# Products that nobody reads, put into the waits of the first stage of a three-part kernel

## The chip, the cores and the metric

The kernel runs as one program on one core of one Trainium2 chip. The metric is the device time of one execution in microseconds (us). TensorE (PE) multiplies, VectorE (DVE), ScalarE (ACT) and GpSimd (POOL) work elementwise, SyncE (SP) issues nearly all DMAs. PE's clock has two levels, 1.2 and 2.4 GHz; the profile gives the granted clock as a share of the higher one, so 0.50 is the lower level.

## The reference

Three parts follow one another, each fed by the one before; all inputs and outputs are float32.

```python
# 1 recurrence: batch 4, heads 8, steps 768, width 48
a = (a_re + i*a_im) * min(|a|, 0.999) / (|a| + 1e-6)
S = a[t] * S + outer(k[t], v[t]);   y[t] = q[t] @ real(S)
# 2 x: 3072 tokens x 384, from y
x = ((x @ w_a) * (x @ w_b)) @ w_out          # 384 -> 1536 -> 384
# 3 routing: 8 experts of 384 -> 1024 -> 384; tokens with x @ w_skip > 0
e = argmax(x @ w_gate);  g = softmax(x @ w_gate)[e]
out = x + g * (relu(x @ w1[e]) @ w2[e])      # the other tokens: out = x
```

## The kernel before

Part 1 is worked in 24 units of 128 time steps of one batch (`units`). A unit has three pieces of code: `att_exp` (logarithm of the magnitude, its running sum as a product with a triangle, exponentials), `att_trig` (phase, its running sum `tp` by a product with a triangle in line 251, sine and cosine, scaled q and k), and `att_pe` (transposes of q and k to `pq` and `pk`, the products `pc`, masked by DVE to `sc`, the output `y` and the state step `ds`). Two units are one group `g` of 256 tokens, of which there are 12.

Part 2 works a group in 12 blocks of 128 hidden columns. `moe1_step(g, f)` is one block: 9 products with w_a and 9 with w_b of 128x128 by 256 columns into the two halves of one bank `ab` of PSUM (lines 506 to 508; tag `ab`, two banks, so a block needs the bank of the block two before it to be read out), then ACT, DVE, ACT and DVE make the two halves `gh` and `gl` of the product, and `moe1_out` adds the block to `op` (lines 490 to 492), two blocks later.

The weights of part 2 arrive in 18 chunks. `decode_w` turns a chunk into float32 (ACT line 378, DVE lines 379, 383, 384), lets POOL release the load of the chunk three further on (`load_after`, line 429), and splits it into a high and a low part (ACT line 389, POOL line 390). For each of the six chunks of w_out it also forms w_out times the gate weights, twice (x = 0, 1): three transposes into a bank `wt` (line 448), ACT copies them out as `wtt` (line 450), three products with the gate weights (line 452) write columns 384 to 394 of the same bank, and DVE copies those to `w2s` (line 453).

The first stage, up to about 150 us, mixes the first units of part 1, the decoding of all chunks and the 12 blocks of group 0. Its program order is the string `START` (`d` a chunk, `e` and `t` the two halves of `att_exps` and `att_trigs`, `m0.3` block 3 of group 0): 

```python
START = 'da0 e0 t0 db1 db0 a do0 da1 do1 m0.0 e1 m0.1 m0.3 da2 m0.2 t1 db2 do2 m0.5 da3 do3 m0.4 db3 da4 l2 m0.7 db4 m0.6 do4 m0.9 do5 m0.8 da5 db5 m0.10 b m1.0 m0.11 e2 t2 m1.4 ...'
```

From this order a planner at build time, with its own estimates of durations, writes the order of each engine: of the instructions that it takes for ready, the earlier traced goes first. `after(later, earlier)` only orders two instructions of one engine. Each engine then runs its list strictly in order; a group of PE products that waits holds up all behind it.

The kernel already has products that nobody reads: two in line 474 behind the first sines (tile `warm`), and in `warm()` (line 666) 10, 6, 24, 13 and 8 of 256 columns, all near 730 to 740 us between part 2 and part 3, made of the bf16 constants `ones` and `iota`.

Of the kernel before, what the change touches and what calls it, by code (L numbers as in the profile page):

```python
# [18 lines left out]
P = 128  # L19
# [30 lines left out]
FILLP = ()  # L50
WARMS = (10, 6, 24)
WARMX = (13, 8)
ENGINES = {getattr(mybir.EngineType, x) for x in ("PE", "Activation", "DVE", "Pool")}
GF = 5
SGN = ()
# [4 lines left out]
def kern(tc, q, k, v, a_re, a_im, w_a, w_b, w_out, w_skip, w_gate, w1, w2, out):  # L60
# [3 lines left out]
    with st:  # L64
# [8 lines left out]
        def bank(tag, name, bufs):  # L73
            return ps.tile([P, 512], F32, tag=tag, name=name, bufs=bufs)

        env = SimpleNamespace(at=("at", "at2"), n=0)

        def at(name):
            env.n += 1
# [157 lines left out]
        def att_trig(i):  # L237
            c, b = units[i]
            d = U[i]
            im = d["im"]  # L240
            t3 = ew.tile([P, W], F32, tag="t3", name=f"t3_{i}")
            t4 = ew.tile([P, W], F32, tag="t4", name=f"t4_{i}")
            tact(out=t4, in_=im, func=AF.Arctan)
            if c > 0:

                cr = ew.tile([1, W], F32, tag="cr", name=f"cr{i}", bufs=1)
                sync.dma_start(cr, carry[b])
                dve.scalar_tensor_tensor(out=t4[:1], in0=cr, scalar=-2.0 * math.pi, in1=t4[:1], op0=ALU.mult, op1=ALU.add)
            tp = at(f"tp_{i}")
            if i < SPL:  # L250
                pe.matmul(tp[:, :W], trit, t4, start=True, stop=True)
            else:
                hi, lo = parts(i, "t", ("t2", "t1"))
                act.activation(out=hi, in_=t4, func=AF.Copy, scale=INV2PI)
                dve.scalar_tensor_tensor(out=lo, in0=t4, scalar=INV2PI, in1=hi, op0=ALU.mult, op1=ALU.subtract)
                cumsum(tp, hi, lo)

            if i in OFF.get("magic", ()):
                act.activation(out=t3, in_=tp[:, :W], func=AF.Identity, bias=b_magic)
            else:  # L260
                dve.tensor_scalar(out=t3, in0=tp[:, :W], scalar1=MAGIC, scalar2=None, op0=ALU.add)
            dve.scalar_tensor_tensor(out=t3, in0=t3, scalar=MAGIC, in1=tp[:, :W], op0=ALU.subtract, op1=ALU.subtract)
            if c + 1 < NCH:
                carry[b] = dpool.tile([1, W], F32, name=f"carry{i}")
                sync.dma_start(carry[b], t3[127:128])
            dve.tensor_scalar(out=t4.bitcast(I32), in0=t3.bitcast(I32), scalar1=0x7FFFFFFF, scalar2=None, op0=ALU.bitwise_and)
            tact(out=t4, in_=t4, func=AF.Sin, scale=-TWO_PI_IN, bias=b_hpi)
            ts = ew.tile([P, W], F32, tag="t1", name=f"ts{i}")
            d["ts"] = ts
            marks["ts", i] = tact(out=ts, in_=t3, func=AF.Sin, scale=-TWO_PI_IN)  # L270
            for nm in ("q", "k"):
                tag = "krl" if nm == "k" and i >= 6 and i % 2 else nm + "r"
                r = ew.tile([P, 2 * W + 32], F32, tag=tag, name=f"{nm}r{i}", bufs=1)
                if nm == "k":
                    pool.memset(r[:, 2 * W :], 0.0)
                    d["kf"] = r
                r = r[:, : 2 * W].rearrange("t (h x d) -> t h x d", x=2, d=D)
                src = d[nm].rearrange("t (h d) -> t h d", d=D)
                off(nm + "c", i).tensor_tensor(out=r[:, :, 0], in0=src, in1=t4.rearrange("t (h d) -> t h d", d=D), op=ALU.mult)
                e = off(nm + "s", i)  # L280
                ins = e.tensor_tensor(out=r[:, :, 1], in0=src, in1=ts.rearrange("t (h d) -> t h d", d=D), op=ALU.mult)
                if e is dve:
                    mark((nm + "r", i), ins)
                d[nm + "r"] = r

        xts = {}

        def att_pe(i):
# [2 lines left out]
            qr, kr, vt, ee = d["qr"], d["kr"], d["v"], d["ee"]  # L291
            sc, qT = [], []
            stt = state[b]
            def delta(prev=None):

                ds = at(f"ds{i}")
                for h in range(H):
                    for x in range(2):
                        l = d["kf"][:, 96 * h + 64 * x : 96 * h + 64 * x + 64]
                        ins = pe.matmul(ds[64 * x : 64 * x + 64, h * D : (h + 1) * D], l, vt[:, h * D : (h + 1) * D], start=True, stop=True).ins  # L300
                        if prev is not None:
                            after(ins, prev)
                        prev = ins
                return ds, prev
# [9 lines left out]
            for hh in range(2):  # L314
                pq = at(f"pq{i}_{hh}")
                for j in range(4):
                    pe.transpose(pq[:96, j * P : (j + 1) * P], qr[:, 4 * hh + j].rearrange("t x d -> t (x d)"), ident)  # L317
                tq = ew.tile([96, 512], F32, tag="tq", name=f"tq{i}_{hh}", bufs=2)
                mark(("tq", i, hh), act.activation(out=tq, in_=pq[:96], func=AF.Copy))
                pk = at(f"pk{i}_{hh}")  # L320
                for j in range(4):
                    pe.transpose(pk[:96, j * P : (j + 1) * P], kr[:, 4 * hh + j].rearrange("t x d -> t (x d)"), ident)  # L322
                tk = ew.tile([96, 512], F32, tag="tk", name=f"tk{i}_{hh}", bufs=2)
                mark(("tk", i, hh), act.activation(out=tk, in_=pk[:96], func=AF.Copy))
                pc = at(f"pc{i}_{hh}")
                for j in range(4):
                    last = pe.matmul(pc[:, j * P : (j + 1) * P], tk[:, j * P : (j + 1) * P], tq[:, j * P : (j + 1) * P], start=True, stop=True).ins  # L327
                s_ = ew.tile([P, 4, P], F32, tag="sc", name=f"sc{i}_{hh}", bufs=2)
                msk = mark(("sc", i, hh), dve.tensor_tensor(out=s_, in0=pc.rearrange("s (j t) -> s j t", t=P), in1=tri[:, None, :].to_broadcast([P, 4, P]), op=ALU.mult))
                sc.append(s_)  # L330
                qT.append(tq)
# [37 lines left out]
            if c + 1 < NCH:  # L369
                new_state(ds)  # L370
            del U[i]


        def decode(dst, raw, by_pool, k):
# [57 lines left out]
        def decode_w(k, dec, wtp, ahead=None):  # L432
            nm, f = chunks[k]
            dd = dec(f"dec{nm}{f}")
            d = dd.rearrange("p (c f) -> p c f", c=2 if nm == "o" else NCC)
            decode(d, env.raw.pop((nm, f)), k in SGN, k)
            if ahead:
                load_after(k + ahead, dd)
            t = env.wpool.tile([P, 2, 2, WO] if nm == "o" else [P, 2, NCC, 2 * P], F32R, tag=f"w{nm}{f}", name=f"w{nm}{f}")
            env.w[nm, f] = t  # L440
            split(*((t[:, x, :, :DM] if nm == "o" else t[:, x] for x in range(2))), d)
            if nm != "o":
                return
            w2 = env.mp.tile([P, 2, 10], F32, tag="w2", name=f"w2s{f}", bufs=2)
            for x in range(2):
                pt = bank("at2", f"wt{f}_{x}", 2)
                for c in range(NCC):
                    pe.transpose(pt[:, c * P : (c + 1) * P], d[:, x, c * P : (c + 1) * P], ident)
                wt = wtp.tile([P, DM], F32, tag="cr", name=f"wtt{f}_{x}", bufs=1)
                act.activation(out=wt, in_=pt[:, :DM], func=AF.Copy)  # L450
                for c in range(NCC):
                    pe.matmul(pt[:, DM : DM + 10], wt[:, c * P : (c + 1) * P], wg[:, c], start=c == 0, stop=c == NCC - 1)
                dve.tensor_copy(w2[:, x], pt[:, DM : DM + 10])
            split(t[:, 0, :, DM:], t[:, 1, :, DM:], w2)

        def att_exps(p):
            table("natural_log_exp_and_others")
# [8 lines left out]
        def att_trigs(p):  # L466
            table("trig_and_small")
            for i in (2 * p, 2 * p + 1):
                att_trig(i)
            if p == 0 and WARM:  # L470

                wm = bank("op", "warm", 2)
                for x in range(WARM):
                    pe.matmul(wm[:, :DM], ident, U[0]["ts"], start=True, stop=True)
            for i in (2 * p, 2 * p + 1):
                att_pe(i)


        M = {}
# [18 lines left out]
        def moe1_step(g, f):  # L498
            xt = M[g][0]
            fs = slice((f % 2) * P, (f % 2 + 1) * P)  # L500
            ab = bank("ab", f"ab{g}_{f}", 2)
            for x, nm in enumerate("ab"):
                o = ab[:, x * 256 : (x + 1) * 256]
                for c in range(NCC):
                    wh, wl = (env.w[nm, f // 2][:, y, c, fs] for y in range(2))
                    pe.matmul(o, wl, xt[:, c, 0], start=c == 0, stop=False)  # L506
                    pe.matmul(o, wh, xt[:, c, 1], start=False, stop=False)  # L507
                    pe.matmul(o, wh, xt[:, c, 0], start=False, stop=c == NCC - 1)  # L508
            if len(pend) == 2:
                moe1_out(*pend.pop(0))  # L510
            asb = env.mp.tile([P, 256], F32, tag="asb", name=f"asb{g}_{f}")
# [146 lines left out]
            if last:  # L658
                warm("t", ins.ins, WARMS[2])

        def warm(name, ins, n):

            if n:
                wm = bank("op", f"warm{name}", 2)
                for x in range(n):
                    after(pe.matmul(wm[:, :CAP], ones, iota, start=True, stop=True).ins, ins)

        giu = cpool.tile([P, 2, NE], U32, name="giu")
        siu = cpool.tile([P, 2, NE], U32, name="siu")
# [241 lines left out]
        moe1_flush()  # L911
        att_next(2)
        env.at = ("at", "at2")
        for g in range(2, NG):
            if g + 1 < NG:
                att_exps(g + 1)
# [186 lines left out]
```

## Time and profile before

| | us |
|---|---|
| median of 3 runs | 890.77 |
| lowest, highest | 889.37, 890.77 |
| the profiled execution, its own time | 892.15 |
| span of its profile, first to last instruction | 890.2 |
| PE busy in the span | 832.7 (94%) |
| DVE, ACT, POOL busy | 560.0, 466.0, 268.3 |

The profiled execution took 1.95 us more than its span, and 1.4 us more than the median. "Idle before" with an arrow names what an engine waited for; L506 is line 506.

### The profile page before, as it was taken

The page shows a single profiled execution, that of the slowest core. Times are in us where ns is not written, and L with a number is a line of the kernel's source. Part 1 is how long each engine was busy: PE and PEld are TensorE (multiplying, and loading weights), DVE is VectorE, ACT ScalarE, POOL GpSimd, SP SyncE. Part 2 cuts the span into 40 slices and gives each one's busy share as a digit, 9 for nine tenths or more (in the row PEclk, how much of TensorE's full clock was granted, in tenths as well). Part 3 has the DMA queues.
Part 4 walks back from the last instruction along what each step waited for, and adds up shares of the span by engine and source line. Part 5 has one row for each costly group of instructions (what it writes and reads, how often), then busy time and mean ns, then how long its engine had stood idle before and what let it go on. Part 6 is the DMA issues. An engine that isn't in the chain of part 4 may idle for free.

```text
span 890.2 us, 18349 instructions
## 1 busy us (share of the span) xinstructions
PE 832.7 (94%) x7051; PEld 804.1 (90%) x7051; DVE 560.0 (63%) x1323; ACT 466.0 (52%) x971; POOL 268.3 (30%) x313
## 2 busy tenths in 40 slices
PE   2578888999999999999999999999999999999995
PEld 0458788999999999999999999999999989999995
DVE  3788986857758385674957749484653644755551
ACT  5576655645647375573745647265443424555540
POOL 5254464114130031310213121031301304676751
PEclk9987987999999999999999999999999999999998
DMA  9869672222223131230312213121101408777600
GB/s 164 162 128 176 158 138 55 72 43 74 47 64 63 28 82 37 72 64 19 90 39 65 60 33 89 33 60 22 55 1 55 133 36 307 244 219 230 194 20 30
DMA packets 162801, 81.53 MB, mean 92 GB/s; under 512 B 132789, under 2 KB 148731, under 8 KB 162705
## 3 DMA queue, kind: packets, MB, share of 16 engines
q1 hardware_dynamic: 160656, 74.88, 35.4%
q0 software_dynamic: 2048, 5.40, 1.7%
q8 instruction: 57, 0.93, 0.5%
q14 instruction: 40, 0.32, 0.1%
HBM read 66.10 MB, written 12.61 MB: 88 GB/s over the span
## 4 chain that ended last, share of the span: by engine, by line
PE 82%; DVE 7%; DMA 5%; ACT 2%; issue 1%; SPq 1%; POOL 1%; POOLq 0%; DVEq 0%; ACTq 0%
PE ab L506 11%; PE ab L508 11%; PE ab L507 11%; PE op L490 5%; PE op L491 5%; PE op L492 5%; PE pc L327 4%; PE y L349 4%; PE eh L783 3%; PE eh L784 2%; PE eh L786 2%; PE eo L800 2%; PE eo L802 2%; PE eo L801 2%; PE pq L317 2%; PE pk L322 2%
## 5 line engine op out<-in xcount | busy, mean ns | idle before, releaser
L506 PE MATMUL ab<-xt,wa 128*128 128x256 f32 x432 | 127.1, 294 | 3.0 <-POOL wa L390 1.2
L506 PE MATMUL ab<-xt,wb 128*128 128x256 f32 x432 | 123.6, 286 | 1.1 <-POOL v L181 1.1
L508 PE MATMUL ab<-xt,wa 128*128 128x256 f32 x432 | 124.1, 287 | 0.0
L507 PE MATMUL ab<-xt,wa 128*128 128x256 f32 x432 | 123.8, 287 | 0.0
L508 PE MATMUL ab<-xt,wb 128*128 128x256 f32 x432 | 123.5, 286 | 0.0
L507 PE MATMUL ab<-xt,wb 128*128 128x256 f32 x432 | 123.0, 285 | 0.0
L513 DVE TENSOR_TENSOR asb<-ab,asb 128x256 f32<-128x256 f32 x144 | 60.3, 418 | 87.8 <-ACT asb L512 86.8
L490 PE MATMUL op<-wo,gl 128*128 128x394 f32 x288 | 100.3, 349 | 2.4 <-DVE gl L517 1.7
L492 PE MATMUL op<-wo,gh 128*128 128x394 f32 x288 | 99.3, 345 | 0.0
L491 PE MATMUL op<-wo,gh 128*128 128x394 f32 x288 | 99.1, 344 | 0.0
L512 ACT ACTIVATE asb<-ab 128x256 f32<-128x256 f32 x144 | 54.2, 376 | 84.6 <-PE ab L508 83.0
L515 ACT ACTIVATE gh<-asb 128x256 fp32r<-128x256 f32 x144 | 59.8, 415 | 67.0 <-DVE asb L513 66.7
L506 PEld LDWEIGHTS ab<-xt,wa 128*128 128x128 f32 x432 | 83.6, 193 | 6.3 <-issue 2.0
L517 DVE TENSOR_TENSOR gl<-asb,gh 128x256 fp32r<-128x256 f32 x144 | 64.1, 445 | 34.3 <-ACT gh L515 34.3
L751 POOL TENSOR_TENSOR wq<-stg,wq 128x768 fp32r<-128x768 f32 x32 | 59.4, 1858 | 85.1 <-DMA xt<-xt 44.0
L507 PEld LDWEIGHTS ab<-xt,wa 128*128 128x128 f32 x432 | 83.8, 194 | 0.0
L508 PEld LDWEIGHTS ab<-xt,wa 128*128 128x128 f32 x432 | 83.6, 194 | 0.2 <-issue 0.2
L506 PEld LDWEIGHTS ab<-xt,wb 128*128 128x128 f32 x432 | 82.2, 190 | 1.7 <-POOL v L181 1.3
L508 PEld LDWEIGHTS ab<-xt,wb 128*128 128x128 f32 x432 | 82.2, 190 | 0.3 <-issue 0.3
L507 PEld LDWEIGHTS ab<-xt,wb 128*128 128x128 f32 x432 | 82.3, 190 | 0.2 <-issue 0.2
L790 DVE SCALAR_TENSOR_TENSOR hl<-eh,hh 128x256 fp32r<-128x256 f32 x64 | 27.1, 424 | 52.2 <-ACT hh L789 52.2
L789 ACT ACTIVATE hh<-eh 128x256 fp32r<-128x256 f32 x64 | 24.6, 384 | 66.8 <-PE eh L786 65.1
(231 smaller groups left out, 2177.1 us busy)
## 6 DMA issues: line engine op xcount, KB each, us to landing
stg<-in_moe_w_dram SPq DMA_DIRECT2D x28, 768.0 KB, 4.5
re<-in_a_re_dram SPq DMA_DIRECT2D x24, 192.0 KB, 2.7
v<-in_v_dram SPq DMA_DIRECT2D x24, 192.0 KB, 2.7
k<-in_k_dram SPq DMA_DIRECT2D x24, 192.0 KB, 3.3
q<-in_q_dram SPq DMA_DIRECT2D x24, 192.0 KB, 2.9
rawo<-in_moe_w_out_dram SPq DMA_DIRECT2D x6, 768.0 KB, 4.4
xd<-xr SPq DMA_DIRECT2D x24, 192.0 KB, 2.3
out_dram<-xr SPq DMA_DIRECT2D x24, 192.0 KB
```

The costliest lines, as they stand in the source:

```text
L327: last = pe.matmul(pc[:, j * P : (j + 1) * P], tk[:, j * P : (j + 1) * P], tq[:, j * P : (j + 1) * P], start=True, stop=True).ins
L490: pe.matmul(o, gl[:, ts], wh, start=f == 0, stop=False)
L491: pe.matmul(o, gh[:, ts], wl, start=False, stop=False)
L492: i = pe.matmul(o, gh[:, ts], wh, start=False, stop=f == NF - 1)
L506: pe.matmul(o, wl, xt[:, c, 0], start=c == 0, stop=False)
L507: pe.matmul(o, wh, xt[:, c, 1], start=False, stop=False)
L508: pe.matmul(o, wh, xt[:, c, 0], start=False, stop=c == NCC - 1)
L512: act.activation(out=asb, in_=ab[:, :256], func=AF.Copy)
L513: dve.tensor_tensor(out=asb, in0=ab[:, 256:], in1=asb, op=ALU.mult)
L515: act.activation(out=gh, in_=asb, func=AF.Copy)
L517: dve.tensor_tensor(out=gl, in0=asb, in1=gh, op=ALU.subtract)
L751: lo.tensor_tensor(out=o[:, 1], in0=t, in1=o[:, 0], op=ALU.subtract)
```

## The change

It adds products that nobody reads in four places and a flag `busy` that is on through the first stage only.

- Behind the phase sum of unit 1 (`tp`, line 251): 60 products of 256 columns in an `op` bank (`warm("c")`), traced ahead of `att_pe` of units 0 and 1.
- Behind the first transpose of unit 0: 40 products of the triangle with itself, 128 columns (`warm("d")`), traced behind all of `att_pe(0)`.
- In each of the 12 passes through line 448: 5 products of 112 columns into columns 400 to 512 of the `wt` bank behind the transposes, and 5 more behind the gate product.
- Ahead of blocks 0, 3 and 9 of group 0: 8, 12 and 10 products of 256 columns into the block's own `ab` bank. They are ordered behind `env.last`: the last product of the block traced before, and for block 0 the gate product of the first chunk of w_out.

Nothing is removed. `START`, the holds and all other code stay.

```diff
+WARMA = (60, 40)
+WARMT = (5, 5)
+WARMB = {'ab0': 8, 'ab3': 12, 'ab9': 10}
@@ decode_w
                 for c in range(NCC):
-                    pe.transpose(pt[:, c * P : (c + 1) * P], d[:, x, c * P : (c + 1) * P], ident)
+                    ins = pe.transpose(pt[:, c * P : (c + 1) * P], d[:, x, c * P : (c + 1) * P], ident).ins
+                if env.busy:
+                    fill(pt, WARMT[0], ins)
...
+                if env.busy:
+                    fill(pt, WARMT[1], ins)
+                    if f == 0:
+                        env.last = ins
                 dve.tensor_copy(w2[:, x], pt[:, DM : DM + 10])
...
+        def fill(b_, n, ins, col=400, w_=112):
+            for x in range(n):
+                after(pe.matmul(b_[:, col : col + w_], ones, iota[:, :w_], start=True, stop=True).ins, ins)
@@ att_trigs
             for i in (2 * p, 2 * p + 1):
-                att_trig(i)
+                ins = env.last = att_trig(i)
+            if p == 0:
+                warm("c", ins, WARMA[0])
...
-                att_pe(i)
+                ins = att_pe(i)
+                if i == 0:
+                    warm("d", ins, WARMA[1], tri_r, tri_r)
@@ moe1_step
             ab = bank("ab", f"ab{g}_{f}", 2)
+            if g == 0 and env.busy:
+                fill(ab, WARMB.get(f"ab{f}", 0), env.last, 0, 256)
...
-                    pe.matmul(o, wh, xt[:, c, 0], start=False, stop=c == NCC - 1)
+                    env.last = pe.matmul(o, wh, xt[:, c, 0], start=False, stop=c == NCC - 1).ins
```

## Rows read from the trace of the kernel before

**Rows 1.** The page, chain that ended last, shares by engine.

```profile
PE 82%; DVE 7%; DMA 5%; ACT 2%; issue 1%; SPq 1%; POOL 1%; POOLq 0%; DVEq 0%; ACTq 0%
```

**Rows 2.** Busy by stretch: PE, PEld, DVE, ACT, POOL; then clock, DMA share, GB/s.

```profile
150.00:850.00 700.00, 695.96 (x6128) 683.32 (x6127) 434.28 (x1125) 365.61 (x785) 178.38 (x202) 1.00 0.31 85
```

**Rows 3.** The same view cut where the granted clock changes in the first stage.

```profile
71.00:74.40 3.40, 1.46 (x13) 1.26 (x11) 3.40 (x4) 1.62 (x3) 2.03 (x2) 1.00 1.01 201
74.40:84.60 10.20, 8.52 (x40) 8.05 (x41) 10.16 (x23) 9.10 (x18) 3.89 (x5) 0.50 1.02 158
...
118.80:125.70 6.90, 5.79 (x27) 5.76 (x28) 6.87 (x9) 4.33 (x10) 6.90 (x6) 0.51 0.44 122
...
139.60:149.80 10.20, 9.47 (x38) 9.47 (x39) 5.39 (x11) 6.75 (x14) 6.54 (x10) 0.52 0.19 40
```

**Rows 4.** PE's instructions in order, 17 to 40 us: start, length, line, count, idle.

```profile
17.11 2.93 PE L251 MATMUL tp<-t,trit 128*128 128x384 f32 x4 [2.80 <-ACT t L153]
25.95 2.93 PE L474 MATMUL warm<-ts,ident 128*128 128x384 f32 x4 [5.91 <-ACT ts L153]
31.31 1.09 PE L317 MATMUL pq<-ident,qr 128*96 128x128 f32 x4 [2.43 <-DVE qr L279]
...
37.03 2.07 PE L327 MATMUL pc<-tq,tk 96*128 96x128 f32 x8 [2.67 <-ACT tk L324]
38.90 1.06 PE L322 MATMUL pk<-ident,kr 128*96 128x128 f32 x4
```

**Rows 5.** Waits of DVE and of ACT, 28 to 57 us: total, times, longest.

```profile
DVE sc L329 <- PE pc L327: 2.9, 1, 2.9
...
ACT tk L324 <- PE pk L322: 2.5, 1, 2.5
```

**Rows 6.** PE's instructions in order, 65 to 89 us.

```profile
65.86 0.55 PE L506 MATMUL ab<-xt,wa 128*128 128x256 f32 x1 [0.23 <-DMA xt<-xt]
...
67.28 0.87 PE L452 MATMUL wt<-wg,wtt 128*128 128x10 f32 x6
...
75.14 0.90 PE L448 MATMUL wt<-ident,deco 128*128 128x128 f32 x3 [2.68 <-DVE w2s L453]
...
79.72 0.56 PE L506 MATMUL ab<-xt,wa 128*128 128x256 f32 x1
...
87.31 1.05 PE L327 MATMUL pc<-tq,tk 96*128 96x128 f32 x8
```

**Rows 7.** DVE's instructions in order, 77 to 89 us.

```profile
77.32 0.41 DVE L513 TENSOR_TENSOR asb<-ab,asb 128x256 f32<-128x256 f32 x1
...
88.41 0.69 DVE L329 TENSOR_TENSOR sc<-pc,tri_r 128x512 f32<-128x512 f32 x1 [2.99 <-PE pc L327]
```

**Rows 8.** The chain that ended last, 84 to 140 us: start, length, what.

```profile
110.94 4.79 DMA rawb<-in_moe_w_b_dram
...
127.88 6.91 DMA rawa<-in_moe_w_a_dram
```

**Rows 9.** PE's instructions in order, 137 to 149 us.

```profile
137.23 0.84 PE L452 MATMUL wt<-wg,wtt 128*128 128x10 f32 x6 [1.75 <-ACT wtt L450]
...
140.33 0.70 PE L490 MATMUL op<-wo,gl 128*128 128x394 f32 x1 [1.65 <-DVE gl L517]
...
144.88 0.56 PE L506 MATMUL ab<-xt,wa 128*128 128x256 f32 x1
...
148.65 0.41 PE L508 MATMUL ab<-xt,wb 128*128 128x256 f32 x1
```

**Rows 10.** Instructions of POOL, SP's queue and ACT in order, 140 to 150 us.

```profile
140.93 1.85 POOL L390 TENSOR_TENSOR wa<-deca,wa 128x768 fp32r<-128x768 f32 x1 [0.77 <-ACT wa L389]
...
142.08 3.69 SPq L368 DMA_DIRECT2D xt<-xt  x6
...
149.16 0.38 ACT L512 ACTIVATE asb<-ab 128x256 f32<-128x256 f32 x1 [1.82 <-PE ab L508]
```

**Rows 11.** PE's products that nobody reads, between part 2 and part 3.

```profile
733.64 2.78 PE L666 MATMUL warmt<-iota,ones 128*128 128x256 bf16 x24
```

More of the change, by code (lines that the diff above doesn't have):

```diff
@@ L74, in bank @@
             return ps.tile([P, 512], F32, tag=tag, name=name, bufs=bufs)
-        env = SimpleNamespace(at=("at", "at2"), n=0)
+        env = SimpleNamespace(at=("at", "at2"), n=0, busy=True)
         def at(name):
@@ L250, in att_trig @@
             if i < SPL:
-                pe.matmul(tp[:, :W], trit, t4, start=True, stop=True)
+                last = pe.matmul(tp[:, :W], trit, t4, start=True, stop=True).ins
             else:
+                last = None
                 hi, lo = parts(i, "t", ("t2", "t1"))
@@ L284, in att_trig @@
                 d[nm + "r"] = r
+            return last
         xts = {}
@@ L293, in att_pe @@
             stt = state[b]
+            first = None
             def delta(prev=None):
@@ L316, in att_pe @@
                 for j in range(4):
-                    pe.transpose(pq[:96, j * P : (j + 1) * P], qr[:, 4 * hh + j].rearrange("t x d -> t (x d)"), ident)
+                    ins = pe.transpose(pq[:96, j * P : (j + 1) * P], qr[:, 4 * hh + j].rearrange("t x d -> t (x d)"), ident).ins
+                    first = first or ins
                 tq = ew.tile([96, 512], F32, tag="tq", name=f"tq{i}_{hh}", bufs=2)
@@ L371, in att_pe @@
             del U[i]
+            return first
         def decode(dst, raw, by_pool, k):
@@ L451, in decode_w @@
                 for c in range(NCC):
-                    pe.matmul(pt[:, DM : DM + 10], wt[:, c * P : (c + 1) * P], wg[:, c], start=c == 0, stop=c == NCC - 1)
+                    ins = pe.matmul(pt[:, DM : DM + 10], wt[:, c * P : (c + 1) * P], wg[:, c], start=c == 0, stop=c == NCC - 1).ins
+                if env.busy:
+                    fill(pt, WARMT[1], ins)
+                    if f == 0:
+                        env.last = ins
                 dve.tensor_copy(w2[:, x], pt[:, DM : DM + 10])
             split(t[:, 0, :, DM:], t[:, 1, :, DM:], w2)
+        def fill(b_, n, ins, col=400, w_=112):
+            for x in range(n):
+                after(pe.matmul(b_[:, col : col + w_], ones, iota[:, :w_], start=True, stop=True).ins, ins)
         def att_exps(p):
@@ L659, in slots, with warm @@
                 warm("t", ins.ins, WARMS[2])
-        def warm(name, ins, n):
+        def warm(name, ins, n, l=None, r=None):
             if n:
@@ L665, in warm @@
                 for x in range(n):
-                    after(pe.matmul(wm[:, :CAP], ones, iota, start=True, stop=True).ins, ins)
+                    o = wm[:, :CAP] if l is None else wm[:, :P]
+                    after(pe.matmul(o, ones if l is None else l, iota if l is None else r, start=True, stop=True).ins, ins)
         giu = cpool.tile([P, 2, NE], U32, name="giu")
@@ L913, in kern @@
         env.at = ("at", "at2")
+        env.busy = False
         for g in range(2, NG):
```

## The prediction

> **What bounds the kernel now.** I read the shares of the chain that ended last first: 82% of it is PE [rows 1]. The view by stretch then says where: from 150 to 850 us PE is busy 695.96 of 700 us at granted clock 1.00 [rows 2]. Whatever brings PE to its 150 us mark earlier is therefore kept to the end, and nothing before that mark counts unless it moves it. So the question is what sets the mark.
>
> The same view cut at the changes of clock shows three stretches at half speed: 74.4 to 84.6, 118.8 to 125.7 and 139.6 to 149.8 [rows 3]. Each follows a pause of PE: 2.68 us ahead of the transposes at 75.14 [rows 6], 1.65 us ahead of the products at 140.33 [rows 9]. A fourth shows in durations alone. The clock column has 1.00 for the first 50 us, but eight products `pc` take 2.07 us at 37.03 [rows 4] and 1.05 us at 87.31 [rows 6], so PE is at the lower level there too.
>
> Which of these are on the chain? At 88.41 DVE had waited 2.99 us for `pc` [rows 7], which PE reached late because it worked at half speed from 79.72. From there the chain goes over DVE to a load of weights at 110.94, then over ACT and POOL to a last load, begun at 127.88 and landed at 134.79 [rows 8], over DVE, and at 140.33 back to PE, which works 9.47 of 10.2 us at half speed [rows 3]. So half speed is paid in full at the end, partly around 80 us, and not at all at 118.8: there PE only has to be done before a load that lands at 134.79.
>
> **Prices.** 24 products of 256 columns that nobody reads took 2.78 us, the last of them 0.27 us in length, so one costs (2.78 - 0.27) / 23 = 0.109 us at full speed [rows 11]. At half speed the 18 products of a block start from 144.88 to 148.65, 0.22 us each [rows 9]. By columns, 112 cost 0.048 or 0.097 us and 128 cost 0.055 or 0.11 us (estimates).
>
> **Behind the first phase sums: 60 and 40.** The sums end at 17.11 + 2.93 = 20.04. PE then idles 5.91 us, runs the two old warm products, idles 2.43 us, and transposes at 31.31 [rows 4]. The cover is 8.3 us. The 60 cost 6.5 us at full and 13.2 us at half speed; the planner takes them ahead of the transposes, since they are traced first. How soon does the clock rise? The three stretches lasted 6.9 to 10.2 us [rows 3]; with the shortest laid from the start of the sums at 17.11, it rises at 24.0 (an estimate): 18 products at 0.22 and 42 at 0.109 end at 28.6, the two old ones then take half of 2.93, and at 30.1 PE is ahead of the transposes: nothing lost. If it never rose, they would end at 33.2 + 2.93 = 36.2, 4.9 us late. I take the first, since the sums already kept PE working for 2.93 us. The 40 products of 128 columns are traced behind all of `att_pe(0)`, so the planner puts them only where it sees PE idle; the pause ahead of `pc` is 2.67 us [rows 4], and they cost 2.2 or 4.4 us. Hidden at full speed; up to 1.7 us late at half.
>
> The gain: at full speed `pc` is 1.0 us and `pk` about 0.5 us shorter. ACT waited 2.5 us for that `pk` and DVE 2.9 us for `pc` [rows 5], so between 0 and 2.4 us can come out there. Of what comes out, ACT and DVE hand on a part. **-1.0 us** taken, bounds -2.4 and +4.9.
>
> **Around the transposes of the output weights: 12 times 5 and 5.** 120 products, 5.8 us at full and 11.6 us at half speed. They lie on two paths. On PE they matter only where PE is late. On the way from transposes over ACT to `w2s` they matter everywhere, because reading a bank waits for all products into it: ACT reads only the first half of `ab`, yet idled 1.82 us until 149.16, past the end of the last product into the second half at 149.06 [rows 9, 10]. So each pass is 0.24 us longer at ACT and 0.24 us at DVE (0.48 at half speed). Behind ACT's copy all its queue waits (the decoding and the splits of weights), behind DVE's copy the next decode step. Twelve passes in a stage where DVE is seldom idle would cost up to 5.8 us if all lay on the chain; the rows show PE's results waiting for DVE instead (the 2.68 us at 75.14 [rows 6]), so I take 0 here and count the two passes on PE's own path below.
>
> **Ahead of block 0: 8.** They are ordered behind the gate product at 67.28, while block 0 began at 65.86 [rows 6]. So block 0 starts later by 1.4 us and by the products' 0.9 to 1.8 us, less the gate product, which now goes first. Cover: the pause of 2.68 us ahead of 75.14, which ends with DVE, not PE. Cost 0; without cover 2.3 us. They also shorten that pause, after which the clock fell.
>
> **Ahead of block 3: 12.** They need the bank of block 0, which DVE has read at 77.32 + 0.41 = 77.73 [rows 7], and stand in front of 79.72 [rows 6], on the way to the `pc` for which DVE waits. Full speed from there saves half of 79.72 to 84.6, 2.4 us, and pays 12 x 0.109 = 1.3 and 0.24 for a pass: -0.9. If the clock rises at 84.6 as before, 12 of the block's own products move behind it: +1.3 and 0.24, +1.6. If the rise is put off by as much as is added, 12 x 0.22 and two fives at half speed: +3.6. Nothing in the trace decides between the first two; I take **0**, bounds -0.9 and +3.6.
>
> **Ahead of block 9: 10.** 1.1 or 2.2 us, before the stretch at 118.8 that the load at 127.88 covers. 0; 2.2 without cover.
>
> **The end of the stage.** Here the clock falls at 139.6, and PE had little to do ahead of it: a gate product at 137.23 behind a pause of 1.75 us, a few more products, a pause of 1.65 us [rows 9]. Two fives of the new products come into just this stretch, 0.5 us. If the clock holds, the work from 140.33 to 144.88 shrinks to 2.3 us, but block 10 needs POOL's part of its weights at 140.93 + 1.85 = 142.78 [rows 10]: 2.1 us won, then half of 144.88 to 149.8, another 2.4. Against that stands a five behind the gate product in this stretch, 0.24 us. So -4.3 us; less if the next block in PE's list is of group 1, whose `xt` is still being issued up to 142.08 + 3.69 = 145.77 [rows 10]: then some 2 us of it go into that wait, -2.3 us. If it doesn't hold: +0.5 us. I take **-3.6 us**, nearer to the larger, since the only wait that the rows show there is the one for 142.78.
>
> **Sum.** -1.0 + 0 + 0 + 0 - 3.6 = -4.6 us on the profiled execution's own 892.15: 887.55. The median lies 1.4 us below that execution, so 886.2 us.
>
> **Rivals.** (1) The clock at the end isn't held: ten short products are little in a stretch with 3.4 us of pauses, and at 71.0 to 74.4 PE was busy 1.46 of 3.4 us and the clock still fell [rows 3]. Then -1.0 + 0.5: 890.2 us. (2) The change doesn't do what it says: PE runs a list that the planner wrote by its own estimates, so the products may stand where PE was busy anyway, not in the pauses, and the clock falls as before; PE pays only what lies on its path at the end, 0.2 to 0.5 us: 891.2. (3) Slower: the products ahead of block 3 run at half speed and put `pc` off. Place: between DVE's read of block 0's bank at 77.73 and `pc`. It decides if the clock is low when that bank comes free and rises no sooner for it. Price +3.6, with the end not held +0.5 and the early gain of 1.0 kept: 893.9. For it: the clock was 0.50 from 74.4 [rows 3]. Against it: the later start of block 0 may put off that fall. (4) All half-speed time comes back.
>
> The three stretches hold 27.3 us, half of which is 13.7 us: 877.1 us. The chain speaks against it, as PE is not on it at 118.8. The Trainium skill (TensorE: Matmul & The Clock Gate, "HAM oscillation") counts it that way: the loss is the throttled time times one half. By that rule the sum would be these 13.7 us; the trace bears it out for the last stretch alone, where PE is busy 9.47 of 10.2 us.
>
> **How the numbers follow.** Forecast 0.48 (its own range 883.5 to 888.7), end not held 0.19, not what it says 0.06, slower 0.23, all comes back 0.04. A measurement of this kernel tells about 0.2% (1.8 us) from no change. Faster: the forecast, the last rival and a little of the first, 0.54; same: the rest of the first and the second, 0.23; slower 0.23. The range reaches from 882.5 (the forecast with -2.4 early, -0.9 at block 3 and -4.3 at the end comes to 883.2) to 893.5, which leaves out the last rival and about half of the slower case.
>
> **What would show it.** Right: a clock of 1.00 through 140 to 150 us and block 10 starting near 143; `pc` of the first unit in 1.05 us; no later transposes than 31.3. Wrong: the 60 still running past 30 us; products ahead of block 3 at 0.22 us each and DVE's wait for `pc` at 88 us above 3 us; the products standing next to busy work; or a load in [rows 8] issued later than before, since then an order changed that I took for unchanged.

## The result and the profile after

| kernel | median us | lowest to highest | ratio to before, 95% interval |
|---|---|---|---|
| before, beside it | 890.37 | 888.65 to 892.14 | |
| after | 900.10 | 894.13 to 901.35 | 1.0085 [1.0066, 1.0103] |

The change makes the kernel slower by 0.85%, 7.6 us by the ratio (the two medians lie 9.7 us apart; this text goes by ratios). The forecast was 4.6 us faster, and 900.1 lies above the range. The profiled execution of after took 898.64 us with a span of 896.7, against 892.15 and 890.2 before. One execution can lie some 6 us off its kernel's median (after itself has one at 894.13), so verdicts below go by the ratios and the profiles only show places.

The page of after, busy time and the chain by engine: PE gained 16.8 us of work, and the chain is PE's as in [rows 1].

```profile
PE 849.5 (95%) x7301; PEld 821.4 (92%) x7301; DVE 558.9 (62%) x1323; ACT 466.3 (52%) x971; POOL 269.0 (30%) x313
PE 83%; DVE 6%; DMA 5%; issue 2%; ACT 1%; POOL 1%; SPq 1%; POOLq 0%; DVEq 0%; ACTq 0%
```

After by stretch, at the cuts of [rows 3] and [rows 2] (columns as there; the clock is the third number from the end):

```profile
71.00:74.40 3.40, 3.40 (x20) 2.96 (x21) 2.93 (x4) 1.70 (x3) 2.75 (x3) 0.50 0.86 183
74.40:84.60 10.20, 8.38 (x75) 7.78 (x74) 10.20 (x19) 6.79 (x14) 4.97 (x5) 0.97 0.81 186
118.80:125.70 6.90, 6.35 (x53) 5.60 (x52) 6.31 (x10) 4.82 (x10) 2.19 (x1) 1.00 0.55 63
139.60:149.80 10.20, 10.20 (x104) 9.88 (x103) 6.84 (x10) 4.67 (x10) 4.89 (x6) 0.82 0.07 15
150.00:850.00 700.00, 695.87 (x6129) 682.83 (x6129) 432.74 (x1124) 367.26 (x790) 181.07 (x204) 1.00 0.32 85
```

This is the striking part. The clock largely did what was hoped: of the three stretches at half speed two are gone and the last is at 0.82; a new one lies at 71.0 to 74.4, at the eight products ahead of block 0. (1 - clock) times length sums to 13.4 us over the four stretches before and to 3.8 us after. These cuts are before's own, and after has a low clock elsewhere too (0.83 from 100 to 110 us, where before has 1.00); from 50 to 150 us as a whole the mean granted clock rises from 0.83 to 0.91, and the sum falls from 17 to 9 us. The kernel is slower all the same. Behind 150 us PE works nearly as it did, so nearly all of the loss was made earlier.

PE of after in order, 17 to 48 us, beside [rows 4]:

```profile
19.80 7.03 PE L692 MATMUL warmc<-iota,ones 128*128 128x256 bf16 x60
26.67 1.46 PE L495 MATMUL warm<-ts,ident 128*128 128x384 f32 x4
31.49 1.09 PE L323 MATMUL pq<-ident,qr 128*96 128x128 f32 x4 [3.36 <-DVE qr L283]
...
34.20 4.94 PE L692 MATMUL warmd<-tri_r 128*128 128x128 f32 x22
38.94 2.02 PE L334 MATMUL pc<-tq,tk 96*128 96x128 f32 x8
...
41.46 4.08 PE L692 MATMUL warmd<-tri_r 128*128 128x128 f32 x18
45.34 2.02 PE L334 MATMUL pc<-tq,tk 96*128 96x128 f32 x8
```

The 60 are hidden and raise the clock: the two old products behind them take 1.46 instead of 2.93 us. Behind a pause of 3.36 us the clock is down again (`pq` 1.09 us). The 40 (`warmd`) come out in two lots, and the second `pc` starts at 45.34 instead of 40.64, where before had

```profile
40.64 2.08 PE L327 MATMUL pc<-tq,tk 96*128 96x128 f32 x8 [0.68 <-ACT tk L324]
```

DVE pays for that; its waits from 28 to 57 us, beside the 2.9 us of [rows 5]:

```profile
DVE sc L336 <- PE pc L334: 6.3, 2, 5.7
```

From there the lateness is handed on. The chain of after between 100 and 130 us has the load of [rows 8] that began at 110.94 now at

```profile
115.45 5.33 DMA rawb<-in_moe_w_b_dram
```

and the last load, which before landed at 134.79 and was copied by ACT from 134.87, is copied from 140.05. ACT and PE of after in order, 134 to 138 us:

```profile
134.66 0.90 ACT L386 ACTIVATE decb<-rawb 128x768 f32<-128x768 f32 x1 [3.73 <-DMA rawb<-in_moe_w_b_dram]
135.46 0.58 ACT L331 ACTIVATE tk<-pk 96x512 f32<-96x512 f32 x1
```

```profile
136.09 1.74 PE L334 MATMUL pc<-tq,tk 96*128 96x128 f32 x8 [2.75 <-ACT tk L331]
```

Before, `tk` ran ahead of `decb`:

```profile
125.65 0.59 ACT L324 ACTIVATE tk<-pk 96x512 f32<-96x512 f32 x1 [1.55 <-PE pk L322]
...
130.74 0.90 ACT L378 ACTIVATE decb<-rawb 128x768 f32<-128x768 f32 x1 [2.95 <-DMA rawb<-in_moe_w_b_dram]
```

After, `decb` stands first in ACT's list and waits for a load, and `tk`, which needs no load, waits behind it, and PE behind that. No part of the diff touches these two. The planner wrote another list: compared place by place, 267 of 1134 instructions of DVE, 204 of 835 of ACT, 43 of 240 of POOL and 79 of 392 of SP stand elsewhere, all in or just behind the first stage. (A block that moves shifts all behind it in its list, so places count high.) PE's own list of the old products is another one too: the lists written out for e2 and e1 below differ in 1042 of the first 1340 places. Even with the ten products ahead of block 9 alone the planner moves 97 of DVE and 68 of ACT. SP's queue shows it in two loads of `xt`, of group 1 (142.08 before [rows 10]) and of group 2, here after's two and then before's second:

```profile
149.75 3.92 SPq L375 DMA_DIRECT2D xt<-xt  x6
...
210.69 3.69 SPq L375 DMA_DIRECT2D xt<-xt  x6
```

```profile
196.87 3.70 SPq L368 DMA_DIRECT2D xt<-xt  x6
```

### The profile page after: what moved, and what is told of

Read it like the earlier page. It is cut to its first block, busy times and chain, and to the rows that moved or that the text cites. A ratio compares the mean times of both kernels' runs of the same rounds, so it can differ in the third digit from the quotient of the medians.

```text
span 896.7 us, 18859 instructions
## 1 busy us (share of the span) xinstructions
PE 849.5 (95%) x7301; PEld 821.4 (92%) x7301; DVE 558.9 (62%) x1323; ACT 466.3 (52%) x971; POOL 269.0 (30%) x313
## 4 chain that ended last, share of the span: by engine, by line
PE 83%; DVE 6%; DMA 5%; issue 2%; ACT 1%; POOL 1%; SPq 1%; POOLq 0%; DVEq 0%; ACTq 0%
PE ab L531 11%; PE ab L533 10%; PE ab L532 10%; PE op L515 5%; PE op L513 5%; PE op L514 5%; PE y L356 5%; PE pc L334 5%; PE eh L809 3%; PE eh L810 2%; PE eh L812 2%; PE eo L826 2%; PE eo L827 2%; PE eo L828 2%; PE pq L323 2%; PE pk L329 2%
## 5 line engine op out<-in xcount | busy, mean ns | idle before, releaser
L531 PE MATMUL ab<-xt,wa 128*128 128x256 f32 x432 | 124.9, 289 | 1.7 <-DMA xt<-xt 1.0
L532 PE MATMUL ab<-xt,wa 128*128 128x256 f32 x432 | 122.3, 283 | 0.0
L533 PE MATMUL ab<-xt,wa 128*128 128x256 f32 x432 | 122.0, 283 | 0.0
L531 PEld LDWEIGHTS ab<-xt,wa 128*128 128x128 f32 x432 | 81.6, 189 | 4.1 <-issue 3.0
L533 PEld LDWEIGHTS ab<-xt,wa 128*128 128x128 f32 x432 | 81.7, 189 | 0.2 <-issue 0.2
L532 PEld LDWEIGHTS ab<-xt,wa 128*128 128x128 f32 x432 | 81.8, 189 | 0.0
```

What stands on the lines that cost most here:

```text
L533: env.last = pe.matmul(o, wh, xt[:, c, 0], start=False, stop=c == NCC - 1).ins
```

## The experiments

So two suspects: the 40 products, and the new order, that of all five engines together (no run takes PE's new list without the others', or the others' without PE's). To part the two, an order was written out: the instructions of each engine, without the new products, are tied one behind the other along a list taken from the program of before or of after.

```diff
+        for o, order_ in zip(made, unpacked(ORDER)):
+            for a, b in zip(order_, order_[1:]):
+                after(o[b], o[a])
```

In these kernels one helper records every operation, so all lines read L68 or L71; tiles tell them apart. The 8 products ahead of block 0 can't stand in the old order (block 0 comes there before the product they are ordered behind) and are left out in all runs named "old order". `before` is measured beside each group of runs, and the ratio is to that.

| run | median us | ratio, 95% interval |
|---|---|---|
| e1 new order, no products | 898.10 | 1.0077 [1.0052, 1.0101] |
| e2 old order, products | 897.75 | 1.0062 [1.0039, 1.0084] |
| e3 old order, without the 40 | 891.13 | 0.9995 [0.9976, 1.0015] |
| e4 the change without the 40 | 898.94 | 1.0082 [1.0060, 1.0105] |
| e5 e1, one place undone | 895.07 | 1.0059 [1.0036, 1.0083] |
| e6 e2, the 40 in bf16 | 889.89 | 1.0005 [0.9986, 1.0024] |
| e7 old order, late products | 890.74 | 0.9995 [0.9977, 1.0013] |
| e8 e7, 14 for 5 in one place | 888.60 | 0.9972 [0.9959, 0.9984] |
| e9 e1, two places undone | 895.88 | 1.0065 [1.0041, 1.0090] |
| e10 after, two places undone | 900.63 | 1.0108 [1.0064, 1.0151] |
| e11 e10, the 40 in bf16 | 895.50 | 1.0055 [1.0034, 1.0075] |
| e12 e8 with the 60 and the 40 in bf16 | 890.75 | 0.9996 [0.9979, 1.0014] |
| e13 new order to 150 us, then old | 897.48 | 1.0073 [1.0050, 1.0096] |
| e14 old order to 150 us, then new | 893.50 | 1.0026 [1.0007, 1.0045] |
| e15 new order to 88 us, then old | 891.53 | 1.0007 [0.9991, 1.0022] |
| e16 old order to 88 us, then new | 895.15 | 1.0055 [1.0034, 1.0076] |
| e17 e6, weights changing | 891.11 | 1.0000 [0.9976, 1.0023] |

### The order or the products

e1 is `before` with the list of after.

> The kernel before, with none of the new products, but every engine's instructions of the first stage put in the order in which the planner left them in the changed kernel (ordering edges alone, taken from the two built programs; the first stage's orders differ in 267 of 1134 places on DVE, 204 of 835 on ACT, 43 of 240 on POOL, 79 of 392 on SP). Theory A (the 40 products of 128 columns stand on the chain at half speed and cost the time, 34.20 to 39.14 and 41.46 to 45.54 us in the changed kernel's trace): the order costs little, 889 to 892 us. Theory B (the planner's new order is what costs): 896 to 901 us.

e2 is `after` with the list of before.

> The new products with every engine held to the order of the kernel before. The 8 ahead of block 0 are left out, since the old order starts block 0 ahead of the gate product that they wait for. Here the planner puts all 40 of the triangle's products into one place, ahead of the first pc. Theory A: 896 to 902 us, with the 40 taking about 8.4 us (0.21 each at half speed) between 34 and 43 us. Theory B: 887 to 892 us.

e3 and e4 take the 40 away, in the old order and in the one that the planner then writes:

```diff
-WARMA = (60, 40)
+WARMA = (60, 0)
```

> As the kernel before in order, with the 60 behind the phase sums, the fives in the wt banks and the 12 and 10 ahead of blocks 3 and 9, but without the 40 of the triangle and the 8 ahead of block 0. Theory A: 886 to 891 us, at or under the kernel before, since nothing else stands on the chain. Theory B gives the same, so it is the difference to the run with the 40 that counts: 6 to 10 us by A, under 2 us by B. If the rest of the products costs by itself (waits of ACT and DVE for the fives), 893 or more.

> The changed kernel without the 40 products of the triangle, everything else as changed, the order left to the planner. Theory A: 888 to 893 us, the larger part of the loss gone. Theory B: 895 to 901 us, unless the planner happens on another order; its trace shows which.

Both suspects hold. The new order, with no product in it, costs about as much as the whole change (e1). The 40 cost 0.67%, 6.0 us, in the old order (e2 against e3). They don't show as a sum in these four runs: e4 is without the 40 and no faster, but its order is a third one. ACT of e1 in order, then PE (at 131 and at 210 us), show the place already seen in after, larger:

```profile
130.28 0.89 ACT L68 ACTIVATE decb<-rawb 128x768 f32<-128x768 f32 x1 [6.01 <-DMA rawb<-in_moe_w_b_dram]
131.06 0.58 ACT L68 ACTIVATE tk<-pk 96x512 f32<-96x512 f32 x1
```

```profile
131.70 2.07 PE L68 MATMUL pc<-tq,tk 96*128 96x128 f32 x8 [5.28 <-ACT tk L68]
...
210.19 2.14 PE L68 MATMUL ab<-xt,wa 128*128 128x256 f32 x15 [0.70 <-DMA xt<-xt]
```

PE's second line is a wait that before has not: the `xt` of group 2 is issued at 206 us.

The two causes leave different marks. The load that began at 110.94 before and at 115.45 in after is not late in e1:

```profile
109.80 5.53 DMA rawb<-in_moe_w_b_dram
```

In the old order it begins at 119.09 with the 40 (e2) and at 111.88 without them (e3). So a late load is the mark of the 40, and in e1 the loss shows as work that stands behind loads.

### The price of the 40

e6 and, later, e17 change only what the 40 multiply, in the old order:

```diff
-                    warm("d", ins, WARMA[1], tri_r, tri_r)
+                    warm("d", ins, WARMA[1], ones, iota[:, :P])
```

> As the run in the old order with all products (897.75 us), but the 40 products behind block 0 of the first unit multiply the bf16 ones by the bf16 ramp instead of the fp32r triangle by itself; columns (128), number and place are the same. Price theory (an fp32r product of 128 columns takes twice what its columns cost a bf16 one): 0.11 us each at the lower clock or 0.055 at the higher instead of 0.21, so 4 to 6 us less ahead of the first pc, which starts near 37.5 instead of 45, and the time falls to 891.5 to 893.5 us. Rival (a product of that length costs 0.21 us whatever its type, or the loss comes from waiting for the bank rather than from the products): within 1 us of 897.75.

PE in order, 33 to 47 us, first of e2, then of e6:

```profile
35.30 8.78 PE L71 MATMUL warmd<-tri_r 128*128 128x128 f32 x40
43.87 2.02 PE L71 MATMUL pc<-tq,tk 96*128 96x128 f32 x8
```

```profile
33.22 3.63 PE L71 MATMUL warmd<-iota,ones 128*128 128x128 bf16 x40
36.68 1.11 PE L71 MATMUL pc<-tq,tk 96*128 96x128 f32 x8
...
45.99 1.04 PE L71 MATMUL pk<-ident,kr 128*96 128x128 f32 x4 [3.39 <-DVE kr L71]
```

The 40 fall from 8.78 to 3.63 us, the clock rises among them, and 0.57% of the time comes back, 5.1 us. But `pc` in half the time wins nothing beyond that: DVE's `kr` comes when it comes, PE now waits 3.39 us for it (0.43 before), and behind that pause `pk` takes 1.04 us again (0.61 before). More came back than the 891.5 to 893.5 us expected. The executions of e2 reach from 891.04 us at a mean granted clock of 0.984 to 900.75 at 0.970, which fits a price that hangs on the clock the 40 meet.

e17 asks whether the type or the loading of weights makes the price: the weights of the 40 alternate between `ones` and `iota`.

> As the run in the old order with the 40 in bf16 (889.89 us, the 40 in 3.63 us), but their weights change from each product to the next between the ones and the ramp. If loading weights is the price: near 0.2 us each at the lower clock again, 6 to 8.5 us for the 40, pc near 41 to 44 and 893 to 897 us. If the type is the price (fp32r at 128 columns): 0.055 to 0.11 us each as before, 888 to 891.5 us.

The groups of `warmd` in after, then in e17 (count, shortest, median and longest in ns, first and last start):

```profile
L692 PEld LDWEIGHTS warmd<-tri_r x40: 333/333/337, 34.1 to 45.0; 128*128 128x128 f32 x40
L692 PE MATMUL warmd<-tri_r x40: 415/415/456, 34.2 to 45.1; 128*128 128x128 f32 x40
```

```profile
L71 PE MATMUL warmd<-iota,ones x20: 314/314/314, 36.5 to 40.6; 128*128 128x128 bf16 x20
L71 PE MATMUL warmd<-iota x20: 314/314/315, 36.6 to 40.7; 128*128 128x128 bf16 x20
```

With changing weights, the 40 still follow each other by (40.7 - 36.5) / 39 = 0.107 us at the lower clock. Changing the bf16 weights costs nothing. Since e6 loads weights for each product too (40 loads of `ones` in its trace), this doesn't part the type's streaming from its loading: what is shown is that 40 products in bf16 are cheap and 40 in fp32r are not.

### Undoing places in the new order

e5 puts `tk` and `wtt` ahead of `decb` again; e9 also puts `sc` of the same half unit on DVE ahead of a copy `w2s`, the last step of `decb` and the first two of `deca`. The places by name:

```diff
 ACT
-decb5, tk3_1, wtt4_1
+tk3_1, wtt4_1, decb5
 DVE
-decb5, decb5, w2s4, decb5, deca5, deca5, sc3_1
+decb5, decb5, sc3_1, w2s4, decb5, deca5, deca5
```

> The kernel before, without any of the new products, on all engines in the order of the kernel after, but for one place on ACT: the copy decb of the last b chunk, which waits for a load, stands behind the copies tk of the last unit's second half and wtt again, as in the kernel before. The same order without this swap took 898.1 us, and there ACT stood still for 6.0 us ahead of decb at 130.28 with pk done at 123.7 and PE idle 5.3 us ahead of pc at 131.70. Theory 1 (this swap is what the new order costs): pc starts near 125.5 and nearly all of the 6 us come back, 892 to 894 us. Theory 2 (the new order loses in many places; PE is held later by the last loads, deca at 135.60 and what follows it, in any case): PE idles elsewhere instead, 896 to 898 us. Between them the swap is a part of it.

> The kernel before, without any of the new products, in the order of the kernel after but for two places: the one on ACT (decb of the last b chunk behind tk and wtt), and one on DVE, where sc of the last unit's second half stands ahead of the last decb step and the first two deca steps, as in the kernel before, instead of behind them. With the first swap alone undone it took 895.07 us (ratio 1.0059), pc was done at 129.1 and PE idled 4.58 us ahead of ds at 137.91, for sc, which DVE made only at 137.18 behind two deca steps of a load landed at 134.71. Theory 1 (the new order costs by work put behind the last loads on ACT and DVE): sc near 132.6, ds near 133.3 in the idle time, 2 to 3.9 us less, 891 to 893.5 us. Theory 2 (the loss is spread, the last load's chain to wa sets block 10 in any case): 894.5 us or more.

e5 moved the wait rather than took it away. PE of e5 in order, 130 to 140 us:

```profile
137.91 1.95 PE L68 MATMUL ds<-v,kr 128*64 128x48 f32 x32 [4.58 <-DVE sc L68]
```

With the first place undone 0.18% came back, which the overlapping intervals can't tell from nothing (1.0077 to 1.0059); with the second, nothing more (1.0065). The theory that these two places are what the order costs has fallen. e10 and e11 undo the same two places in the change itself, e11 with the 40 in bf16:

> The kernel after with all its products and its order, but for the same two places. Theory 1 with the price of the 40 kept (0.21 us each at the lower clock, 22 of them and 18 of them ahead of the two pc of the first unit): what the two places cost comes back, 2 to 5 us of 900.1, 895 to 898 us. Rival (with its products the kernel after is late elsewhere, so the two places don't matter): 899 us or more.

> As the run before this one, but the 40 multiply the bf16 ones by the bf16 ramp. If the order's two places and the price of the 40 are the causes and add up: 4 to 5 us less again, 890.5 to 893 us, that is no different from the kernel before or a little slower. If the 12 products ahead of block 3, the fives or the 8 ahead of block 0 cost as well: 894 to 896 us.

e10 is no better than after. From e10 to e11 0.53% comes back: the price of the 40 is near the same 5 us in the new order as in the old one.

### Where in the order

Four lists are made of the two, cut where before has a certain instruction: the first product of block 0 of group 1 (150 us), or the transposes of w_out's chunk 2 (88 us).

> The kernel before without any new product; all engines in the order of the kernel after for what the kernel before has issued by 150 us, then in the order of before. Theory S (the new order costs in the first stage, by work behind loads): as the whole new order, 1.006 to 1.008 of before, 895 to 898 us. Theory L (it costs behind the stage, by what the planner moved of the second group's attention, whose xt is issued at 205 to 210 instead of 197 us): within 0.2% of before, 889 to 892 us.

> The reverse: the order of before up to 150 us, then that of the kernel after. Theory S: within 0.2% of before, or up to 1 us slower for the 0.7 us in which PE idles at 210 us. Theory L: 1.004 to 1.007 of before, 894 to 897 us.

> The order of the kernel after for what the kernel before has issued by 88 us (its first w_out chunk 2), then the order of before; no new product. In the single profiles both orders had lost the same at 90 us (PE idle or at the lower clock for 49 us of it in either), so by them: within 0.2% of before. If the early loads come in another order and hold the rest up: 1.003 or more.

> The reverse of the run before this: before's order up to 88 us, then that of the kernel after. By the single profiles the whole loss lies behind 90 us (pc behind decb behind a load, 5.3 us of PE idle at 126 to 131; xt of the second group): 1.006 to 1.008 of before, 895 to 898 us. If the halves share it: 1.003 to 1.005.

The first half of the new order costs nothing that can be told (1.0007), the part from 88 us on 0.55%, the part behind 150 us 0.26% alone. That leaves some 0.3% for 88 to 150 us, if parts add. e13 says more than that, but its seam has a wait of its own, which before, after and e1 have not: PE idles 2.23 us ahead of 154.39. Its chain, 149 to 158 us:

```profile
149.72 1.64 ACT t L68 x4
151.38 1.28 ACT L68
...
154.39 3.46 PE ab L68 x18
```

e14 has such a seam as well: PE idles 0.99 us ahead of its block at 151.78, for DVE's `asb`, which stands behind a step that waits 2.46 us for the load of `imp`. So of e14's 0.26%, 2.3 us, its trace names 0.99 for the seam and 0.70 for PE's wait for `xt`. With both seams taken off in full (an estimate), 88 to 150 us cost some 0.4%. Which places there make it up stays open.

### What the late products are worth

In e3, everything but the 40 and the 8 is in the old order, and the time is before's. PE of e3 in order, 81 to 90 us, and two stretches:

```profile
81.17 2.54 PE L71 MATMUL ab<-iota,ones 128*128 128x256 bf16 x12
83.46 1.31 PE L71 MATMUL ab<-xt,wa 128*128 128x256 f32 x9
...
88.88 1.05 PE L71 MATMUL pc<-tq,tk 96*128 96x128 f32 x8
```

```profile
74.40:84.60 10.20, 7.70 (x48) 6.69 (x49) 10.20 (x22) 8.26 (x16) 3.60 (x5) 0.67 1.06 161
...
139.60:149.80 10.20, 9.41 (x65) 9.21 (x63) 7.14 (x12) 7.09 (x15) 7.23 (x11) 0.83 0.16 35
```

The 12 ahead of block 3 run at half speed, the block starts 3.7 us later than before [rows 6], the clock then rises and `pc` is 1.6 us late. So e7 keeps only the late products, and e8 lengthens one group:

```diff
-WARMA = (60, 40)
+WARMA = (0, 0)
-WARMB = {'ab0': 8, 'ab3': 12, 'ab9': 10}
+WARMB = {'ab9': 10}
-                if env.busy:
-                    fill(pt, WARMT[0], ins)
+                if env.busy and f >= 3:
+                    fill(pt, WARMT[0], ins)
...
-                if env.busy:
-                    fill(pt, WARMT[1], ins)
+                if env.busy and f >= 3:
+                    fill(pt, 14 if (f, x) == (5, 0) else WARMT[1], ins)
```

(e7 has WARMT[1] in the last line.)

> The order of the kernel before; of the new products only those of the end of the stage: the fives of the output weights' chunks 3 to 5 and the 10 ahead of block 9; no 60, no 40, none ahead of blocks 0 and 3. Clock theory (what holds the clock at the end of the stage comes from these alone, and what ate the gain in the run without the 40 came from the early ones: 12 products ahead of block 3 at 0.21 us each and the fives ahead of them): clock above 0.75 in 140 to 150, block 10 near 143.5, 888 to 889.5 us against 891.1 without the 40. Rival (late fives pay at the passes of the weights what they win in clock; the stage ends with loads and POOL's splits whatever PE does): within 0.2% of the kernel before, 889.5 to 892.5 us.

> As the run with the late products only, but 14 instead of 5 of the short ones behind the first gate product of the last chunk, so that they reach into the pause of PE that in the run without the 40 lay at 140.26 to 141.05 ahead of op and after which the clock was 0.59. Clock theory: the pause is gone and the clock holds 1.00 through 141 to 144, another 1 to 1.5 us, 886.5 to 888.5 us. Rival (the wait for DVE and POOL there sets op and block 10, and nine more products only delay the copy w2s that DVE makes from their bank): the same as the run with five or up to 1 us more.

PE of e8 in order, 137 to 143 us, and the last stretch, beside [rows 9] and [rows 3]:

```profile
137.46 0.85 PE L71 MATMUL wt<-iota,ones 128*128 128x112 bf16 x14
...
139.51 0.45 PE L71 MATMUL op<-wo,gl 128*128 128x394 f32 x1 [0.32 <-DVE gl L71]
...
142.21 1.30 PE L71 MATMUL ab<-xt,wa 128*128 128x256 f32 x9
```

```profile
139.60:149.80 10.20, 10.16 (x79) 9.99 (x80) 6.79 (x13) 7.74 (x18) 6.29 (x6) 1.00 0.29 59
```

The pause of 1.65 us is 0.32, the clock holds, block 10 starts 2.67 us earlier, and 0.28% is won: e8 beats both kernels, at 888.6 us. With five instead of 14 (e7) no gain over before could be told. e12 adds the 60 and the 40 in bf16 to e8:

> The order of the kernel before with those products that paid: the 60, the 40 in bf16, the late fives of chunks 3 to 5 with 14 behind the first gate product of the last chunk, the 10 ahead of block 9; none ahead of blocks 0 and 3, none around chunks 0 to 2. The late ones alone gave 888.6 us, 0.28% less. If the early clock (pc of the first unit in 1.1 us from 36.7) reaches the end: another 1 to 2 us, 886.5 to 888 us. If the early gain is taken up by the loads that DVE waits for at 46 to 62 us: 888 to 889.5 us.

They take the gain away again, against an expectation of 886.5 to 889.5 us (the intervals of e8 and e12 just touch). PE of e12 in order, 139 to 142 us:

```profile
139.43 1.14 PE L71 MATMUL wt<-wg,wtt 128*128 128x10 f32 x6 [2.88 <-ACT wtt L71]
140.41 1.47 PE L71 MATMUL wt<-iota,ones 128*128 128x112 bf16 x14
```

The gate product comes 2.7 us later than in e8 (136.77 there, behind 1.76 us), and the 14 begin at half speed. Why that pass is late in e12 was not followed further.

## Why the prediction was wrong, step by step

**What bounds the kernel** held: behind 150 us PE is busy 695.87 of 700 us, where before had 695.96, and what the first stage loses reaches the end.

**The step that failed first** is one that the sum did not have. The prediction took the order of all work but the new products for unchanged, because `START` and the holds stay. The planner, though, picks by its own estimates of when an instruction is ready, and 250 more products on PE shift those for every engine. The new lists alone cost 0.77% (e1). The second rival had the planner in it, but only for where the new products would stand; the new order of the old work should have been a rival with a price. The prediction's last part named a sign for a changed order, a load of [rows 8] issued later, and it came: 115.45 for 110.94. It was luck that it pointed right, since the new order alone has that load earlier (109.80, e1), and the 40 in the old order have it later (119.09, e2). Block 0 did show a changed order: behind a product that came after it, it had to move, and where the prediction had it 2 to 3 us later at no cost it starts at 73.87 instead of 65.86 [rows 6]. What that move costs by itself was not tried.

**The 40** were mis-sized and misplaced. The price by columns, 0.11 us at the lower clock, is that of bf16 products; these are fp32r, 0.21 us. And they did not stand only in the pause of 2.67 us: 4.94 us of them stand ahead of the first `pc` and 4.08 ahead of the second, which starts 4.7 us late. The bound of +4.9 had the right size by luck, for another reason (the 60 at half speed); the taken value, -1.0, was wrong. e2 to e6 give 5.1 us and e10 to e11 4.7 us for the type alone.

**The 60** were hidden as forecast (`pq` at 31.49 for 31.31), and ended at 26.8 rather than 28.6. The gain expected from them did not come: a pause of 3.36 us follows, and the clock is low when `pc` needs it. With bf16 products in that gap it was high (e6), and then DVE's `kr` took the gain.

**The 12 ahead of block 3**: rival 3 had the mechanism and the place, and its +3.6 is what block 3 shows in e3 (3.7). At `pc` it was +1.6, the prediction's middle case. In after itself they ran at full speed. Taken 0; not the cause.

**The fives and the 10 ahead of block 9** at 0: the late ones together with the 10 cost nothing (e7), nor do all of them together with the 60 and the 12 (e3). The early fives were not tried by themselves, nor the 8 ahead of block 0.

**The end of the stage**: the mechanism was right, the size not. With the clock held, block 10 starts at 142.21 where "near 143" was forecast, and the time falls by 2.5 us, not 3.6 (e8). With fives alone the clock is 0.83 to 0.88 (e3, e7) and the gain too small to tell.

**All half-speed time comes back** fell, as given a small chance. From 50 to 150 us, (1 - clock) times length is 8 us less in after, and after is 7.6 us slower; in e2 the mean granted clock of that stretch is 0.93, the sum 10 us less, and it is 0.62% slower; e3, whose stretches at 118.8 and 139.6 are at 1.00 and 0.83, is no faster than before. By the rule of the Trainium skill (TensorE: Matmul & The Clock Gate, "HAM oscillation"), throttled time times one half, these 8 and 10 us should have been won. The measurements decide: here the rule counts PE's loss, not the kernel's.

As a sum, by the ratios: the order costs 6.9 us (e1; 5.3 and 5.8 with one and two places undone), the 40 cost 5.1 us for their type alone and 6.0 in all (e2 against e3), and a held clock is worth up to 2.5 us. That would be 8 to 13 us if they added, and 7.6 were measured. With the two places undone they do add, as far as e10's wide interval tells: the order alone costs 0.65% (e9), with all products but the 40 in bf16 0.55% (e11), and with the 40 in fp32r 1.08% (e10), so their type costs 0.53% there and 0.57% in the old order. In the change itself they don't in full: e1 and e2 would make 1.39%, and 0.85% was measured. PE's wait for `tk` ahead of the late `pc` is 5.28 us in e1 and 2.75 us in after, so a part of what the 40 are late may fall into that wait; this is argued from one trace each, and the rest stays open.

## What to carry to other kernels

Where a planner writes the engines' lists, an edit on one engine is an edit to all: compare the lists before and after, that engine's own included, and price the change of order as a term of its own. Fill a pause only up to what is waited for, with the cheapest product there is (bf16, few columns), and only in the pause after which the work is on the chain; here 14 short ones at the end of the stage won 0.28%, and the rest, early ones that repaired the clock elsewhere, gave nothing. Half-speed time off the chain was free here. What a filler is late can be handed on nearly in full over DVE, ACT and loads (e2: the first `pc` 6.8 us later, 6.0 us lost against e3) or not at all (e3: the `pc` at 88 us 1.6 us later, nothing lost).

## What the runs showed of the hardware

A product of 128 columns costs by its type: fp32r 0.21 us at the lower clock ((45.1 - 41.46) / 17 in after's second lot of 18), as much as one of 256 columns in `ab` [rows 9], and bf16 0.107 us, with weights that change (e17) or not (e6: 17 of the 40 start from 33.2 to 34.9). Beside each fp32r one the profile shows a weight load of 0.33 us, beside a bf16 one of 0.15 us (e17), both at the lower clock. The Trainium skill (TensorE: Matmul & The Clock Gate, "Weight-path perf modes — Fast Weight Load (FWL) and DoubleRow") has the fast weight load for types other than FP32. These two loads agree with that if fp32r counts as FP32 there, which the section doesn't say. Whether load or streaming sets the 0.21 us was not tried.

In these traces the clock followed work and pauses: up within 60 products (7.03 us, the old ones behind them at 1.46 for 2.93 us), down behind the 3.36 us pause that follows, up again within the 40 bf16 products of e6, down behind the 3.39 us wait for `kr`.
